# A planned kernel on one core: new load and crossbar times for the planner, a wider spacing of the attention, and batch 1's gates chunk by chunk

## The chip, the core and the metric

The kernel runs on one core of a Trainium2 chip. A core has several engines that work side by side: TensorE (PE in the profile) for matmuls, VectorE (DVE), ScalarE (ACT), GpSimd (POOL) and SyncE (SP), and 16 DMA engines that move data. The metric is the time of one execution on the device, in microseconds (us). The span of the profile is some 1.8 us shorter than that time.

The kernel before takes 193.66 us (median of four runs, 193.41 to 194.00).

## The reference

Four batches, eight heads, 768 steps, head size 48. A gated linear attention feeds an MLP-mixer:

```python
f = 1.0 / (1.0 + np.exp(-f_logit))
for t in range(S):                                     # S = 768
    state = f[:, :, t, :, None] * state + np.einsum('bhd,bhe->bhde', k[:, :, t], v[:, :, t])
    y[:, :, t] = np.einsum('bhd,bhde->bhe', q[:, :, t], state)
x = y, heads side by side                              # (4, 768, 384), shortened here
h = np.maximum(x.transpose(0, 2, 1) @ w_tok1, 0.0) @ w_tok2     # token mixing, 768 -> 256 -> 768
u = x + h.transpose(0, 2, 1)
out = u + np.maximum(u @ w_ch1, 0.0) @ w_ch2                    # channel mixing, 384 -> 1536 -> 384
```

Batch after batch, the kernel does the attention in six chunks of 128 steps and then the mixing. The channel mixing holds most of the matmul time. The attention of batch b + 1 is woven into the mixing of batch b.

## The kernel before

The order of the kernel's operations is not written down by hand. Each operation is handed to a `Plan` with the engine (or the engines) that can do it, the time that it is believed to take, what it waits for, and a priority, `key`. `order()` then plays the whole kernel through with these believed times and yields one list, and the operations are emitted in this order. On the chip each engine's queue works through its own part of the list from front to back. So a believed time changes no arithmetic and no duration. It changes which operation stands before which, on every engine, and which of two possible engines gets an operation.

```python
class Plan:
    # time between the end of an operation and its result being seen elsewhere
    LATE = {"PE": 0.32, "ACT": 0.24, "DVE": 0.24, "POOL": 0.3, "SP": 0.1, "Q": 2.0}
    ...
    def order(self):
        queues = {e: sorted((o for o in self.ops if e in o["eng"]), key=lambda o: o["key"])
                  for e in ("PE", "ACT", "DVE", "POOL", "SP", "Q")}
        ...
        while len(out) < len(self.ops):
            # of each engine: the operation that can start first, among those within
            # 0.02 us of it the one of the smallest key; of all engines, the earliest of these
            ...
            ends[n] = t + o["eng"][e]
            visible[n] = ends[n] + self.LATE[e]
```

"Q" stands for the DMA engines together: one channel on which transfers follow each other. A load by GpSimd is two operations, the issue on GpSimd's queue and the transfer on Q. A crossbar transpose (the DMA engines turn a tile; used in place of a matmul against the identity for q and k from batch 2's fifth chunk on, and for the mixing of batches 2 and 3) is an issue on SyncE and, before the change, 0.7 us on Q too.

```python
def load_f(b, key, at=0.0):           # the gate's input of a whole batch, batches 1 to 3
    m = swdge(lambda e: nc.gpsimd.dma_start(out=f_sb[i], in_=src), key, 2.28, 5.9, 0.3, ...)
def load_qkv(b, c, key, at=0.0):      # q, k, v of one chunk: three loads
    made[name, b, c] = swdge(lambda e, ...: nc.gpsimd.dma_start(...), key, 0.89, 0.71, 1.0, ...)
def crossbar(dst, src, key, deps):
    n = add({"SP": 1.2}, lambda e: nc.sync.dma_start_transpose(out=dst, in_=src), key, deps)
    return add({"Q": 0.7}, None, key, [n])

def gates(b, c0, c1, key):            # of n chunks at once
    cost = 0.08 + 0.33 * n
    a = add({"ACT": cost}, ... Exp ...)                         # profile: L255
    h = add({"ACT": cost}, ... Lhi = Ln, bf16 ...)              # L257
    g = add({"ACT": cost}, ... Ln, fp32 ...)                    # L259
    o = add({"POOL": 0.85 * n, "DVE": 0.4 * n + 0.08},          # Llo, L261: GpSimd or VectorE,
            lambda e: on(e).tensor_tensor(lo, fb, hi, ALU.subtract), key, [g, h])   # as the plan picks

LEAD = (-0.05, 0.11)                  # where attention stands among the mixing's keys
PACE = (33.0, 4.5)                    # attention of chunk m not before 33.0 + 4.5 m us
for b in range(B):
    # loads of batch b + 1 (from b = 1 on)
    ...
    n = 2
    for c in range(0, NCH, n):
        gates(b + 1, c, c + n, b + 0.85 + LEAD[0] + LEAD[1] * c)
        for a in range(c, c + n):
            attention(b + 1, a, b + 1.0 + LEAD[0] + LEAD[1] * a, PACE[0] + PACE[1] * (NCH * b + a))
    mixing(b, b + 1.0, 1.0)
order = plan.order()
```

Lines that the profile names below: L237 a load of q, k or v; L246 the crossbar; L331 the scores (q times k), which need both turned tiles; L371 and L376 the readout; L407 and L426 token mixing; L461 and L480 channel mixing; L188 and L190 copies on ScalarE and VectorE. The tiles: f_sb is the gate, Lhi its negative logarithm in bf16 and Llo the rest that bf16 left out; kh and qh are the scaled k and q, kT and qT the same turned; x_bf is the attention's result, which token mixing reads; u_bf and its turned uT feed the channel mixing, zT is its hidden layer; pA, py, pm and others that begin with p are results of matmuls.

Of the kernel before, what the change touches and what calls it, by code (L numbers as in the profile page):

```python
# [14 lines left out]
class Plan:  # L15



    LATE = {"PE": 0.32, "ACT": 0.24, "DVE": 0.24, "POOL": 0.3, "SP": 0.1, "Q": 2.0}
    BANKS = {"att": 5, "mix": 3}  # L20
    WINDOW = 150

# [3 lines left out]
    def add(self, engines, fn, key, deps=(), bank=None, frees=None, at=0.0, banks=1):  # L26
        n = len(self.ops)
        self.ops.append(dict(n=n, eng=engines, fn=fn, key=(key, n), deps=[d for d in deps if d is not None],
                             bank=bank, banks=banks, readers=[], at=at))
        if frees is not None:  # L30
            self.ops[frees]["readers"].append(n)
            self.ops[n]["deps"].append(frees)
        return n

    def order(self):
        queues = {e: sorted((o for o in self.ops if e in o["eng"]), key=lambda o: o["key"])
                  for e in ("PE", "ACT", "DVE", "POOL", "SP", "Q")}
        free = dict.fromkeys(queues, 0.0)
        ends, visible, on = {}, {}, {}
        taken = {b: [] for b in self.BANKS}  # L40
        out = []

        def earliest(o, e):
            t = max(free[e], o["at"])
            for d in o["deps"]:
                if d not in ends:
                    return None
                t = max(t, ends[d] + 0.05 if on[d] == e and e != "Q" else visible[d])
            if o["bank"]:
                t_ = taken[o["bank"]]  # L50
                k = len(t_) - self.BANKS[o["bank"]]
                for k_ in range(max(k, 0), k + o["banks"]):
                    for r in self.ops[t_[k_]]["readers"]:
                        if r not in ends:
                            return None
                        t = max(t, visible[r])
            return t

        while len(out) < len(self.ops):
            best = None  # L60
            for e, q in queues.items():
                while q and q[0]["n"] in ends:
                    q.pop(0)
                found, seen = [], 0
                for o in q:
                    if o["n"] in ends:
                        continue
                    seen += 1
                    if seen > self.WINDOW:
                        break  # L70
                    t = earliest(o, e)
                    if t is not None:
                        found.append((t, o))
                if not found:
                    continue
                t0 = min(t for t, _ in found)
                t, o = min(((t, o) for t, o in found if t <= t0 + 0.02), key=lambda f: f[1]["key"])
                if best is None or t < best[0]:
                    best = (t, o, e)
            t, o, e = best  # L80
            n = o["n"]
            ends[n] = t + o["eng"][e]
            visible[n] = ends[n] + self.LATE[e]
            on[n] = e
            free[e] = ends[n]
            if o["bank"]:
                taken[o["bank"]] += [n] * o["banks"]
            out.append((t, e, o))
        return out
# [3 lines left out]
def kernel(  # L93
# [12 lines left out]
    nc = tc.nc  # L106
# [30 lines left out]
    w_tok1 = st([128, NCH, DT], BF16, "w_tok1")  # L137
# [7 lines left out]
    f_sb = two([128, H, NCH, D], FP32, "f_sb")  # L145
# [34 lines left out]
    add = plan.add  # L180
    made = {}
# [21 lines left out]
    def swdge(fn, key, cost, us, units, deps, at=0.0):  # L203

        room, ring = 6.5 - units, []
        for m, u in reversed(issued):
            room -= u
            if room < 0:
                ring = [m]
                break  # L210
        n = add({"POOL": cost}, fn, key, list(deps) + ring, at=at)
        m = add({"Q": us}, None, key, [n])
        issued.append((m, units))
        return m

    def load_f(b, key, at=0.0):
        i = b % 2
        src = f_logit[b].rearrange("h (c t) d -> t h c d", t=C)
        if b == 0:
            for c in range(NCH):  # L220

                held = [] if c < 3 else [add({"DVE": 0.07}, lambda e, c=c: nc.vector.memset(
                    f_sb[i][0:1, 0, c, 0:1], 0.0), key + 0.06 * c, [], at=1.9 * c - 0.2)]
                n = add({"SP": 0.05}, lambda e, c=c: nc.sync.dma_start(out=f_sb[i][:, :, c, :], in_=src[:, :, c, :]),
                        key + 0.06 * c, held)
                made["f", b, c] = add({"Q": 1.1}, None, key + 0.06 * c, [n])
        else:
            m = swdge(lambda e: nc.gpsimd.dma_start(out=f_sb[i], in_=src), key, 2.28, 5.9, 0.3,
                      [made.get(("lo", b - 2, c)) for c in range(NCH)], at)
            for c in range(NCH):  # L230
                made["f", b, c] = m

    def load_qkv(b, c, key, at=0.0):
        i = b % 2
        for name, dst, src, users in (("q", q_sb, q, ("qh",)), ("k", k_sb, k, ("kh",)), ("v", v_sb, v, ("y", "d"))):
            made[name, b, c] = swdge(
                lambda e, dst=dst, src=src: nc.gpsimd.dma_start(out=dst[i][:, c], in_=chunk_of(src, b, c)),  # L237
                key, 0.89, 0.71, 1.0, [made.get((u, b - 2, c)) for u in users], at)

    def load_w(name, dst, src, key, us, units):  # L240
        made[name] = swdge(
            lambda e: nc.gpsimd.dma_start(out=dst, in_=src.rearrange("(kt p) n -> p kt n", p=128)),
            key, 0.85, us, units, [])

    def crossbar(dst, src, key, deps):
        n = add({"SP": 1.2}, lambda e: nc.sync.dma_start_transpose(out=dst, in_=src), key, deps)  # L246
        return add({"Q": 0.7}, None, key, [n])

    def gates(b, c0, c1, key):
        i, n = b % 2, c1 - c0  # L250
# [136 lines left out]
    def mixing(b, key0, span):  # L387
        i = b % 2
# [80 lines left out]
        for tt in range(NCH):  # L469
            t = {}  # L470
            kk = key(2.0)
            if b + 1 < B and tt >= NCH - 2:
                kk = key0 + span + 0.12
            half = None
            for k0 in (0, NCC // 2):
                def ch2(e, tt=tt, k0=k0, t=t):
                    if k0 == 0:
                        t["p"] = bank("mix", "pm")
                    for kt in range(k0, k0 + NCC // 2):
                        nc.tensor.matmul(t["p"][:, 0:DM], lhsT=zT[:, kt, tt * 128:(tt + 1) * 128],  # L480
                                         rhs=w_ch2[:, kt, :], start=(kt == 0), stop=(kt == NCC - 1))
                n = add({"PE": 0.99}, ch2, kk,
                        [half, made["w_ch2"]] + [made["z", b, tt // 3, kt] for kt in range(NCC)],
                        bank="mix" if k0 == 0 else None)
                first = n if k0 == 0 else first
                half = n
            made["c2", b, tt] = half
            o = out_sb[tt]
            n = made["o", b, tt] = add({"DVE": 0.47}, lambda e, tt=tt, t=t, o=o: nc.vector.tensor_tensor(  # L489
                o, u_nat[i][:, tt, :], t["p"][:, 0:DM], ALU.add),  # L490
                kk, [half, made.get(("out", tt))], frees=first)
            s = add({"SP": 0.1}, lambda e, tt=tt, o=o: nc.sync.dma_start(out=out_b[tt], in_=o), kk, [n])
            made["out", tt] = add({"Q": 0.7}, None, kk, [s])

    W2 = 5
    FIRST = 0.3
    XBAR_QK = 16
    XBAR_U = 2
    LEAD = (-0.05, 0.11)
    PACE = (33.0, 4.5)  # L500

    load_f(0, 0.0)
    load_qkv(0, 0, 0.0)
# [4 lines left out]
    made["masks"] = add({"POOL": 1.4}, masks, 0.0)  # L508
    for c in range(1, NCH):
        load_qkv(0, c, 0.1 * c)  # L510
    load_w("w_tok1", w_tok1, moe_w_tok1, 0.60, 3.0, 0.75)
    load_w("w_tok2", w_tok2, moe_w_tok2, 0.61, 2.2, 0.25)
    load_f(1, 0.615)
    load_w("w_ch1", w_ch1, moe_w_ch1, 0.62, 6.0, 0.4)
# [7 lines left out]
    for b in range(B):  # L522
        if b + 1 < B:
            for c in range(NCH):
                if b >= 1:
                    if c == 0:
                        load_f(b + 1, b + 0.05)
                    load_qkv(b + 1, c, b + 0.05 + 0.1 * c)
            n = 2
            for c in range(0, NCH, n):  # L530
                gates(b + 1, c, c + n, b + 0.85 + LEAD[0] + LEAD[1] * c)
                for a in range(c, c + n):
                    attention(b + 1, a, b + 1.0 + LEAD[0] + LEAD[1] * a, PACE[0] + PACE[1] * (NCH * b + a))
        mixing(b, b + 1.0, 1.0)
# [43 lines left out]
```

## Time and profile before

| | before |
|---|---|
| time, median of 4 runs | 193.66 us |
| span | 192.0 us |
| PE busy | 170.5 us (89%) |
| first channel-mixing matmul | 42.60 us |
| PE idle, 48 to 162 us | 3.4 us |

The page's first two parts, for the kernel before. Each digit is the busy share, or the granted TensorE clock, in tenths in one of 40 slices of 4.8 us:

```profile
PE 170.5 (89%) x1668; PEld 105.4 (55%) x1668; DVE 129.5 (67%) x286; ACT 129.4 (67%) x292; POOL 81.0 (42%) x92
PE   0787896679999999999999899999998999999992
PEclk9999999957999999999999999999999999999999
```

PE is the bound from the tenth slice on. What it loses lies in the first nine: the attention of batch 0, fed by loads, and then batch 0's token mixing, where the clock falls too. One caution belongs to the clock row: its first record falls where the matmuls become fast, and before it the row shows full clock although the matmuls run at half rate. In this trace the first record is at 24.8 us. The two 128x384 matmuls of a chunk's cumulative sum start 0.27 to 0.30 us apart in batch 0's later chunks, up to 24.1 us, and 0.17 us apart from 48.5 us on.

The stretches by engine, kernel before. The columns are the stretch, its length, the busy time and number of instructions of PE, PEld, DVE, ACT and POOL, the mean granted clock, the mean busy share of the DMA engines (3.15 means 3.15 of 16) and GB/s:

```profile
36.00:42.00 6.00, 3.44 (x28) 1.91 (x27) 5.51 (x10) 5.32 (x9) 4.11 (x3) 0.70 2.04 144
42.00:48.00 6.00, 6.00 (x65) 3.85 (x63) 4.94 (x11) 4.89 (x14) 6.00 (x8) 0.73 1.76 93
...
96.00:102.00 6.00, 6.00 (x77) 3.77 (x76) 5.91 (x14) 5.89 (x14) 5.26 (x7) 1.00 3.15 130
102.00:108.00 6.00, 4.99 (x41) 2.69 (x40) 5.09 (x13) 5.81 (x14) 0.16 (x1) 1.00 2.04 93
108.00:114.00 6.00, 6.00 (x61) 3.70 (x59) 4.47 (x10) 4.62 (x10) 1.48 (x1) 1.00 0.37 74
114.00:120.00 6.00, 6.00 (x48) 3.80 (x47) 3.03 (x6) 1.46 (x3) 0.00 (x0) 1.00 0.42 112
```

Between 36 and 42 us PE works 3.44 of 6 us, at a clock of 0.70. That is the hole which the change is aimed at.

Two pieces of the chain of waits, kernel before (start, duration, what):

```profile
101.08 6.33 DMA kT_92<-kh_88
107.85 1.57 PE pm L461 x9
```

And PE's wait for that transpose in the view of waits (total us, times, longest):

```profile
PE pA_1824 L331 <- DMA kT_92<-kh_88: 0.7, 1, 0.7
```

The transpose took 6.33 us from issue to landing (the median of the kernel's 28 is 2.42).

### The profile page before, as it was taken

The numbers are of one execution on the slowest core, as the hardware profiler recorded it, in microseconds if no ns is written. First come the engines' busy times: TensorE is split into PE (matmuls) and PEld (weight loads), VectorE is DVE, ScalarE is ACT, GpSimd is POOL, SyncE is SP. The second block draws the span as 40 slices with busy tenths as digits, with TensorE's granted clock in tenths as the row PEclk, the third lists the DMA queues.
The fourth block names the chain that finished last, engine by engine and source line by source line (L and its number), as shares of the span: only waits on it lengthen the run. The fifth ranks groups of instructions, "written<-read, shape, count | busy, mean of one in ns | idle before, by whom it ended". The sixth has DMA issues, their size and how long they took to land.

```text
span 192.0 us, 4351 instructions
## 1 busy us (share of the span) xinstructions
PE 170.5 (89%) x1668; PEld 105.4 (55%) x1668; DVE 129.5 (67%) x286; ACT 129.4 (67%) x292; POOL 81.0 (42%) x92
## 2 busy tenths in 40 slices
PE   0787896679999999999999899999998999999992
PEld 0455553346666666656555566565665654656560
DVE  4578888988899757988998973898673637200222
ACT  4999793987989959774899953257996122598000
POOL 7999992199992449993990300000000000000000
PEclk9999999957999999999999999999999999999999
DMA  8999999999999999999999343344532124310222
GB/s 105 162 149 143 141 216 194 196 101 107 112 192 195 167 122 171 180 199 155 180 144 115 58 82 113 103 85 130 84 64 48 41 85 100 78 70 2 81 86 82
DMA packets 102213, 23.23 MB, mean 121 GB/s; under 512 B 95312, under 2 KB 100992, under 8 KB 102192
## 3 DMA queue, kind: packets, MB, share of 16 engines
q0 software_dynamic: 78800, 13.77, 99.6%
q1 hardware_dynamic: 23392, 9.18, 21.1%
q8 instruction: 13, 0.21, 0.5%
q14 instruction: 8, 0.07, 0.1%
HBM read 25.17 MB, written 4.72 MB: 156 GB/s over the span
## 4 chain that ended last, share of the span: by engine, by line
PE 53%; DVE 18%; ACT 15%; DMA 6%; issue 4%; POOL 2%; DVEq 0%; POOLq 0%; ACTq 0%
PE pm L480 24%; PE pm L461 14%; DMA kT_92<-kh_88 3%; PE pm L407 3%; DMA k_sb_72<-in_k_dram 3%; PE pm L426 2%; ACT zT L194 2%; DVE u_bf L190 2%; PE py L371 1%; ACT state_bd_103 L188 1%; DVE Am_96 L337 1%; DVE Am_95 L337 1%; DVE u_nat_109 L430 1%; ACT u_bf L188 1%; ACT state_bd_102 L188 1%
## 5 line engine op out<-in xcount | busy, mean ns | idle before, releaser
L461 PE MATMUL pm<-uT,w_ch_68 128*128 128x384 bf16 x288 | 54.5, 330 | 1.1 <-ACT zT L194 0.8
L480 PE MATMUL pm<-w_ch_69,zT 128*128 128x384 bf16 x288 | 50.5, 326 | 0.0
L194 ACT ACTIVATE zT<-pm 128x384 bf16<-128x384 f32 x73 | 34.7, 500 | 6.2 <-PE pm L461 5.8
L480 PEld LDWEIGHTS <-zT 128*128 128x128 bf16 x288 | 27.3, 98 | 17.7 <-issue 0.4
L461 PEld LDWEIGHTS <-w_ch_68 128*128 128x128 bf16 x288 | 26.3, 98 | 17.2 <-issue 2.6
L237 POOL DMA_DIRECT2D k_sb_72<-in_k_dram x12 | 11.0, 920 | 4.9 <-DMA f_sb_76<-in_f_logit_dram 4.9
L237 POOL DMA_DIRECT2D q_sb_70<-in_q_dram x12 | 11.2, 932 | 4.4 <-DMA w_ch_69<-in_moe_w_ch_dram 3.6
L196 DVE TENSOR_SCALAR zT<-pm 128x384 bf16<-128x384 f32 x23 | 12.2, 551 | 1.2 <-PE pm L461 1.2
L237 POOL DMA_DIRECT2D k_sb_73<-in_k_dram x12 | 11.2, 932 | 3.7 <-DVE zT L196 3.7
L426 PE MATMUL pm<-h1T,w_tok_67 128*128 128x384 bf16 x48 | 10.9, 332 | 0.8 <-ACT h1T L194 0.4
L237 POOL DMA_DIRECT2D v_sb_75<-in_v_dram x12 | 11.3, 941 | 0.0
L237 POOL DMA_DIRECT2D v_sb_74<-in_v_dram x12 | 11.1, 926 | 0.4 <-issue 0.4
L237 POOL DMA_DIRECT2D q_sb_71<-in_q_dram x12 | 11.2, 936 | 0.0
L261 POOL TENSOR_TENSOR Llo_81<-f_sb_77,Lhi_79 128x768 bf16<-128x768 f32 x3 | 5.0, 1669 | 14.7 <-ACT f_sb_77 L259 14.7
L489 DVE TENSOR_TENSOR out_sb_114<-u_nat_110,pm 128x384 f32<-128x384 f32 x2 | 1.1, 550 | 14.1 <-PE pm L480 14.1
L274 PE MATMUL pS<-Lhi_78,tri_bf 128*128 128x384 bf16 x12 | 4.9, 409 | 4.8 <-POOL ident masks.py:197 4.8
L188 ACT CAST x_bf_106<-py 128x384 bf16<-128x384 f32 x10 | 4.8, 482 | 6.4 <-PE py L376 6.4
L190 DVE COPY x_nat_105<-py 128x384 f32<-128x384 f32 x8 | 4.5, 558 | 6.5 <-ACT x_bf_107 L188 6.4
L188 ACT CAST x_bf_107<-py 128x384 bf16<-128x384 f32 x8 | 3.9, 488 | 7.3 <-PE py L376 7.2
L190 DVE COPY x_nat_104<-py 128x384 f32<-128x384 f32 x9 | 5.0, 558 | 5.4 <-ACT x_bf_106 L188 5.4
L287 ACT ACTIVATE G_82<-pS 128x384 bf16<-128x384 f32 x12 | 5.9, 488 | 4.2 <-PE pS L281 4.1
L430 DVE TENSOR_TENSOR u_nat_109<-x_nat_104,pm 128x384 f32<-128x384 f32 x12 | 6.2, 550 | 3.6 <-PE pm L426 3.5
(237 smaller groups left out, 394.8 us busy)
## 6 DMA issues: line engine op xcount, KB each, us to landing
f_sb_77<-in_f_logit_dram POOLq DMA_DIRECT2D x2, 1152.0 KB, 12.1
f_sb_76<-in_f_logit_dram SPq DMA_DIRECT2D x6, 192.0 KB, 4.5
q_sb_70<-in_q_dram POOLq DMA_DIRECT2D x12, 96.0 KB, 5.7
k_sb_72<-in_k_dram POOLq DMA_DIRECT2D x12, 96.0 KB, 5.2
v_sb_74<-in_v_dram POOLq DMA_DIRECT2D x12, 96.0 KB, 5.2
w_ch_68<-in_moe_w_ch_dram POOLq DMA_DIRECT2D x1, 1152.0 KB, 15.5
q_sb_71<-in_q_dram POOLq DMA_DIRECT2D x12, 96.0 KB, 7.9
k_sb_73<-in_k_dram POOLq DMA_DIRECT2D x12, 96.0 KB, 6.1
```

What stands on the lines that cost most here:

```text
L188: nc.scalar.copy(dst, src)
L190: on(e).tensor_copy(dst, src)
L194: nc.scalar.activation(dst, src, AF.Relu, bias=0.0, scale=1.0)
L196: nc.vector.tensor_scalar(dst, src, 0.0, None, ALU.max)
L237: lambda e, dst=dst, src=src: nc.gpsimd.dma_start(out=dst[i][:, c], in_=chunk_of(src, b, c)),
L261: lambda e: on(e).tensor_tensor(lo, fb, hi, ALU.subtract), key, [g, h])
L287: return lambda e: nc.scalar.activation(dst.rearrange("t h d -> t (h d)"), t["pS"][:, 0:DM], AF.Exp, bias=0.0, scale=scale)
L407: nc.tensor.matmul(t["p"][:, 0:DM], lhsT=w_tok1[:, kt, rt * 128:(rt + 1) * 128], rhs=x_bf[i][:, kt, :], start=(kt == 0), stop=(kt == NCH - 1))
L426: nc.tensor.matmul(t["p"][:, 0:DM], lhsT=w_tok2[:, kt, tt * 128:(tt + 1) * 128], rhs=h1T[:, kt, :], start=(kt == 0), stop=(kt == 1))
L430: u = made["u", b, tt] = add({"DVE": 0.47}, lambda e, tt=tt, t=t: nc.vector.tensor_tensor(u_nat[i][:, tt, :], x_nat[i][:, tt, :], t["p"][: ...
L461: nc.tensor.matmul(t["p"][:, 0:384], lhsT=w_ch1[:, kt, cc * 128:(cc + 1) * 128], rhs=uT[:, kt, th * 384:(th + 1) * 384], start=(kt == 0), ...
L480: nc.tensor.matmul(t["p"][:, 0:DM], lhsT=zT[:, kt, tt * 128:(tt + 1) * 128], rhs=w_ch2[:, kt, :], start=(kt == 0), stop=(kt == NCC - 1))
```

## The change

Its intent is to let the planner believe what the profile measured (loads and crossbar), and to close the hole in batch 0's token mixing: batch 1's gates, which were done two chunks at a time in the middle of it, go chunk by chunk and later.

```diff
-    LATE = {"PE": 0.32, "ACT": 0.24, "DVE": 0.24, "POOL": 0.3, "SP": 0.1, "Q": 2.0}
+    LATE = {"PE": 0.32, "ACT": 0.24, "DVE": 0.24, "POOL": 0.3, "SP": 0.1, "Q": 2.0, "X": 1.3}
-                  for e in ("PE", "ACT", "DVE", "POOL", "SP", "Q")}
+                  for e in ("PE", "ACT", "DVE", "POOL", "SP", "Q", "X")}
     # load_f
-            m = swdge(..., key, 2.28, 5.9, 0.3,
+            m = swdge(..., key, 2.28, 6.3, 0.3,
     # load_qkv
-                key, 0.89, 0.71, 1.0, ...
+                key, 0.89, 0.78, 1.0, ...
     # crossbar
-        return add({"Q": 0.7}, None, key, [n])
+        return add({"X": 0.1}, None, key, [n])
     # store of the output
-            s = add({"SP": 0.1}, ...
+            s = add({"SP": 0.45}, ...
-    LEAD = (-0.05, 0.11)
-    PACE = (33.0, 4.5)
+    LEAD = (-0.05, 0.13)
+    PACE = (34.0, 5.6)
-    load_w("w_tok1", w_tok1, moe_w_tok1, 0.60, 3.0, 0.75)
+    load_w("w_tok1", w_tok1, moe_w_tok1, 0.60, 3.3, 0.75)
-            n = 2
+            n = 2 if b else 1
-                gates(b + 1, c, c + n, b + 0.85 + LEAD[0] + LEAD[1] * c)
+                gates(b + 1, c, c + n, b + (0.85 if b else 0.95) + LEAD[0] + LEAD[1] * c)
```

Below, its four parts have letters: **D**, the load times (f, q/k/v, w_tok1); **X**, the crossbar on a channel of its own, with its latency and the store's cost; **P**, LEAD and PACE; **G**, the gates of batch 1.

More of the change, by code (lines that the diff above doesn't have):

```diff
@@ L227, in load_f @@
         else:
-            m = swdge(lambda e: nc.gpsimd.dma_start(out=f_sb[i], in_=src), key, 2.28, 5.9, 0.3,
+            m = swdge(lambda e: nc.gpsimd.dma_start(out=f_sb[i], in_=src), key, 2.28, 6.3, 0.3,
                       [made.get(("lo", b - 2, c)) for c in range(NCH)], at)
@@ L237, in load_qkv @@
                 lambda e, dst=dst, src=src: nc.gpsimd.dma_start(out=dst[i][:, c], in_=chunk_of(src, b, c)),
-                key, 0.89, 0.71, 1.0, [made.get((u, b - 2, c)) for u in users], at)
+                key, 0.89, 0.78, 1.0, [made.get((u, b - 2, c)) for u in users], at)
     def load_w(name, dst, src, key, us, units):
@@ L491, in mixing @@
                 kk, [half, made.get(("out", tt))], frees=first)
-            s = add({"SP": 0.1}, lambda e, tt=tt, o=o: nc.sync.dma_start(out=out_b[tt], in_=o), kk, [n])
+            s = add({"SP": 0.45}, lambda e, tt=tt, o=o: nc.sync.dma_start(out=out_b[tt], in_=o), kk, [n])
             made["out", tt] = add({"Q": 0.7}, None, kk, [s])
```

## The prediction

> **What bounds it now.** TensorE: the page gives PE 170.5 us busy of 192.0 (89%), VectorE and ScalarE 67% each; the chain of waits is 53% PE. In stretches of 6 us PE is full from 48 us on: 3.4 us idle until 162 us, nothing until 188, then a tail of 3.7 us. What is lost lies before: 0 to 32 us (batch 0's attention, fed by loads; nearly unchanged) and 32 to 46 us, batch 0's token mixing. There, by stretches of 1 us, PE idles 3.7 us (32 to 42), and the granted clock is 0.72, 0.50 for six microseconds, then 0.86: 3.4 us of clock lost. The Trainium skill ("TensorE: Matmul & The Clock Gate", Part 1) says that the clock halves after an idle window of about 3.4 us; the trace agrees: the drop follows 35 to 38 us with PE 0.48, 0.54, 0.33 busy.
>
> **Why that hole.** Batch 1's gates come in blocks of two chunks, 0.83 us an instruction on ScalarE. The timeline shows nine of them from 34.0 to 42.4 us, 7.3 us of work, before or between the copies that token mixing needs. f for batch 1 landed at 34.0 us, and ScalarE stood 0.9 us waiting for it: the planner had believed it earlier. VectorE carries the mixing almost alone (u_nat, u_bf, uT; one u_bf took 1.74 us while GpSimd ran Llo). The first channel-mixing matmul starts at 42.6 us, though token mixing's second product began at 33.2.
>
> **What changes.** No arithmetic goes. (a) Loads are believed 10% slower and f 0.4 us slower, so batch 1's f is planned about 2 us later: copies come first. (b) Batch 1's gates go in single chunks (0.52 us alone, about 0.43 in a row) with later keys; they cost ScalarE some 0.5 us more in all, but block no copy for 0.8 us. (c) The crossbar gets its own channel: in the trace 1.2 us of SyncE each and 2.4 us to landing, 6 us where it met loads at 101 us; it was planned near 4. (d) Attention is paced 5.6 us a chunk in place of 4.5, away from 42 to 66 us (ScalarE and VectorE 80 to 98% busy) towards emptier stretches (114 to 126 us: ScalarE 1.5 to 2.4 of 6).
>
> **What it is worth.** Token mixing's own work is about 4 us on each of two engines plus 2 us of latency, so the first channel matmul should start near 38.5 to 39.5 us: 3 to 4 us gained (estimate from the durations above). If PE stays warm, 1.5 us more. Later stages hold at most 3.4 us; I expect between +0.5 and -1 us there, as the postponed gates load a nearly full ScalarE, and a crossbar planned too early makes PE wait. Sum: -4.7 us.
>
> **Prediction:** 189.2 us, 8 in 10 between 186.5 and 192.2. Faster by over 2% (below 190.0) 0.57, within 2% 0.40, slower 0.03.
>
> **What would show it.** First channel-mixing matmul at or before 39.5 us; mean granted clock between 36 and 48 us above 0.85 (now 0.72); ScalarE's gates between 34 and 40 us halved; PE busy down 2 to 4 us, since cold matmuls go; first crossbar transpose later than 97.6 us; batch 3's last readout (148 us) not earlier; idle PE between 48 and 162 us unchanged within 1.5 us.
>
> **What would make it wrong.** The clock drops all the same, as token mixing alone keeps PE half busy. The hole moves: batch 1's attention starts late and ScalarE, with the gates, bounds 44 to 66 us. Late pacing leaves too little work to cover batch 3's token mixing near 150 to 160 us. Or a reordered head loses what the mixing wins.

## More of the kernel before

GpSimd's timeline near 100 us, kernel before (start, duration, engine, line, operation; in brackets the idle time before it and what ended it):

```profile
99.43 0.96 POOL L237 DMA_DIRECT2D k_sb_73<-in_k_dram  x1
100.30 0.97 POOL L237 DMA_DIRECT2D v_sb_75<-in_v_dram  x1
107.84 1.64 POOL L261 TENSOR_TENSOR Llo_81<-f_sb_77,Lhi_79 128x768 bf16<-128x768 f32 x1 [6.58 <-ACT f_sb_77 L259]
```

The last loads of batch 3's q, k and v are issued by 101.3 us. GpSimd then waits 6.58 us for ScalarE before its next Llo (of batch 3's chunks 2 and 3; the one of chunks 0 and 1 ran on VectorE, at 101.54 us), and nothing stands behind it. A wait like this costs nothing.

## The result and the profile after

| | before | after |
|---|---|---|
| time, median of 4 runs | 193.66 us | 203.20 us |
| range | 193.41 to 194.00 | 202.74 to 203.27 |
| span | 192.0 us | 201.0 us |
| first channel-mixing matmul (L461) | 42.60 us | 44.42 us |
| mean clock, 36 to 48 us | 0.72 | 0.86 |
| PE idle, 102 to 120 us | 1.0 us | 5.4 us |
| last readout with the state (L376) | 151.9 us | 161.8 us |

The ratio is 1.049 (95% interval 1.046 to 1.051): the change is slower by 4.9%. Here and below, a ratio is the mean time of one kernel's fast runs over that of the other's fast runs in the same rounds, so it is not quite the ratio of the medians.

The first parts of the page, kernel after (slices of 5.0 us):

```profile
PE 174.6 (87%) x1668; PEld 106.8 (53%) x1668; DVE 132.8 (66%) x295; ACT 127.3 (63%) x295; POOL 80.3 (40%) x92
PE   0687797879999999989977499999899999999992
PEclk9999999699999999999999579999999999999999
```

The dip of the clock in the mixing is smaller (one slice at 6 in place of 5 and 7), and a new hole stands in slices 21 to 23, with the clock low behind it. The same stretches as above, kernel after:

```profile
36.00:42.00 6.00, 5.17 (x33) 2.74 (x33) 5.12 (x12) 4.46 (x12) 0.91 (x1) 0.72 1.92 169
42.00:48.00 6.00, 4.95 (x59) 3.28 (x56) 5.81 (x14) 6.00 (x18) 5.46 (x7) 1.00 1.35 73
...
96.00:102.00 6.00, 6.00 (x77) 3.81 (x76) 5.24 (x11) 5.28 (x11) 0.91 (x1) 1.00 0.43 20
102.00:108.00 6.00, 4.55 (x43) 2.60 (x41) 5.89 (x13) 4.77 (x12) 6.00 (x8) 1.00 1.63 68
108.00:114.00 6.00, 2.07 (x24) 1.14 (x22) 2.18 (x7) 2.98 (x7) 4.25 (x4) 0.79 2.21 117
114.00:120.00 6.00, 6.00 (x35) 3.18 (x34) 3.84 (x8) 2.89 (x6) 0.00 (x0) 0.64 0.52 52
```

Between 102 and 120 us PE idles 1.45 + 3.93 = 5.38 us, and the clock takes 2.07 x 0.21 + 6.00 x 0.36 = 2.59 us more: 7.97 us, against 1.01 us before. So 7.0 of the 9.0 us of span are lost in these 18 us.

To place the rest, I added up the matmul work issued by a given time, each matmul counted with its full-clock stream time (0.163 us for 384 columns, 0.056 for 128, 0.043 for 96, 0.025 for 48 and less). The kernel after is behind by 2.1 us at 36 us, by 0.1 at 48, by 0.7 at 102, by 7.7 at 120 and by 8.8 at 180. In words: the head lost 2.1 us, the token mixing won 2.0 us, the hole took 7.0 us, and 1.7 us went elsewhere.

**The head.** The attention of batch 0 was no aim of the change, but it got later. The last copy of batch 0's attention on ScalarE, kernel before and kernel after, in the timeline:

```profile
31.79 0.48 ACT L188 CAST x_bf_106<-py 128x384 bf16<-128x384 f32 x1 [0.72 <-PE py L376]
```

```profile
35.52 0.48 ACT L188 CAST x_bf_106<-py 128x384 bf16<-128x384 f32 x1 [3.08 <-PE py L376]
```

The token-mixing matmuls around it show that TensorE had become fast by 28 us before (4 matmuls in 0.82 us) and not after (5 in 1.81 us). First the kernel before, then the kernel after:

```profile
28.09 0.82 PE L407 MATMUL pm<-x_bf_106,w_tok_66 128*128 128x384 bf16 x4
```

```profile
28.95 1.81 PE L407 MATMUL pm<-x_bf_106,w_tok_66 128*128 128x384 bf16 x5
```

**The hole.** GpSimd's timeline, kernel after:

```profile
93.63 0.89 POOL L237 DMA_DIRECT2D v_sb_75<-in_v_dram  x1
101.09 1.63 POOL L261 TENSOR_TENSOR Llo_81<-f_sb_77,Lhi_79 128x768 bf16<-128x768 f32 x1 [6.56 <-ACT f_sb_77 L259]
102.67 0.92 POOL L237 DMA_DIRECT2D q_sb_71<-in_q_dram  x1
...
109.64 0.96 POOL L237 DMA_DIRECT2D v_sb_75<-in_v_dram  x1
```

In the new plan the Llo of batch 3's first two chunks stands on GpSimd in front of nine loads of q, k and v. The planner believed that ScalarE's Ln for it would be done at 95.9 us; ScalarE, busy 5.28 of the 6 us from 96 to 102, started it at 100.14. So GpSimd stood 6.56 us, and the nine loads behind it stood too. The Trainium skill says in "TensorE: Matmul & The Clock Gate" (section "Architectural detail") that ScalarE and VectorE are strict first-in-first-out queues, and GpSimd one for each of its cores; this trace agrees: no load went past the waiting Llo. The DMA engines are nearly empty from 96 to 102 us (0.43 of 16, 20 GB/s; before 3.15 and 130 GB/s). The loads that should have run then are issued from 102.67 to 110.6 us and meet the crossbar transposes of batch 2's last chunks. From the chain of waits, kernel after:

```profile
106.45 0.31 DVE zT L196
106.76 6.47 DMA kT_92<-kh_88
...
113.89 0.43 PE pm L461
```

And the wait for it, kernel after:

```profile
PE pA_1836 L331 <- DMA kT_92<-kh_88: 3.9, 1, 3.9
```

A landing of 6.47 us is no news: before it was 6.33. New is that PE's queue now had the scores right behind the transposes, because the planner believed the turned tile to be there 2.7 us after the start of the issue (1.2 for the issue, 0.1 until it is seen, 0.1 on X, 1.3 until that is seen). Before, it was 4.0 us (1.2 + 0.1 + 0.7 + 2.0) plus whatever was queued on Q. PE ran out of work at 109.35 us and stood until 113.28:

```profile
108.70 0.65 PE L461 MATMUL pm<-uT,w_ch_68 128*128 128x384 bf16 x3
113.28 0.29 PE L331 MATMUL pA_1836<-qT_90,kT_92 48*128 48x128 bf16 x1 [3.93 <-DMA kT_92<-kh_88]
```

The clock then fell to half for 6.8 us, from 111.5 us on. The Trainium skill ("TensorE: Matmul & The Clock Gate", Part 1) gives an idle window of about 3.4 us, 3413 ns, as the cause of a fall. The length agrees: the low phases in the clock records of all traces last multiples of 3.41 us, but for the last of each trace, which the end cuts off. That the window must be idle does not agree: this fall came 2.1 us after PE ran out of work, and PE had been busy 38% of the 3.41 us before it. The fall at 38.45 us in the kernel before, of which the prediction speaks, followed 3.41 us with PE busy 44%.

The late Llo slowed VectorE too. The Trainium skill ("SBUF — State Buffer", section "Who interferes with whom") says that a VectorE instruction with two inputs in SBUF contends with a GpSimd instruction that reads SBUF, and this trace agrees: the state update (L358), normally 0.36 us, took 1.79 us at 101.14 us, while Llo ran 1.63 us from 101.09. 1.31 us of it stand on the chain of waits.

So far this is a reading of one trace. Two causes, the held loads and the early scores, are named in it, and experiments were made to tell them apart.

### The profile page after: what moved, and what is told of

Its sections match the earlier page's. It is cut to its first block, busy times and chain, and to the rows that moved or that the text cites. A ratio compares the mean times of both kernels' runs of the same rounds, so it can differ in the third digit from the quotient of the medians.

```text
span 201.0 us, 4327 instructions
## 1 busy us (share of the span) xinstructions
PE 174.6 (87%) x1668; PEld 106.8 (53%) x1668; DVE 132.8 (66%) x295; ACT 127.3 (63%) x295; POOL 80.3 (40%) x92
## 4 chain that ended last, share of the span: by engine, by line
PE 53%; DMA 15%; DVE 14%; ACT 10%; issue 3%; POOL 3%; DVEq 0%; POOLq 0%; ACTq 0%
PE pm L480 24%; PE pm L461 13%; DMA f_sb_77<-in_f_logit_dram 6%; PE pm L407 4%; DMA kT_92<-kh_88 3%; ACT zT L194 3%; DMA k_sb_72<-in_k_dram 2%; PE py L371 2%; DMA k_sb_73<-in_k_dram 2%; PE pm L426 2%; DMA kT_93<-kh_89 2%; DVE Am_97 L337 2%; PE py L376 2%; DVE u_nat_109 L430 1%; DVE Am_95 L337 1%
## 5 line engine op out<-in xcount | busy, mean ns | idle before, releaser
L461 PE MATMUL pm<-uT,w_ch_68 128*128 128x384 bf16 x288 | 54.3, 333 | 0.4 <-ACT zT L194 0.2
L480 PE MATMUL pm<-w_ch_69,zT 128*128 128x384 bf16 x288 | 51.7, 330 | 0.0
L194 ACT ACTIVATE zT<-pm 128x384 bf16<-128x384 f32 x68 | 32.4, 496 | 11.0 <-PE pm L461 10.7
L461 PEld LDWEIGHTS <-w_ch_68 128*128 128x128 bf16 x288 | 26.4, 99 | 17.1 <-issue 2.3
L196 DVE TENSOR_SCALAR zT<-pm 128x384 bf16<-128x384 f32 x28 | 14.9, 549 | 2.2 <-PE pm L461 2.2
L426 PE MATMUL pm<-h1T,w_tok_67 128*128 128x384 bf16 x48 | 11.6, 361 | 0.8 <-ACT h1T L194 0.4
L261 POOL TENSOR_TENSOR Llo_81<-f_sb_77,Lhi_79 128x384 bf16<-128x384 f32 (+1 forms) x4 | 5.2, 1293 | 17.7 <-ACT f_sb_77 L259 17.7
L489 DVE TENSOR_TENSOR out_sb_114<-u_nat_110,pm 128x384 f32<-128x384 f32 x2 | 1.1, 552 | 14.1 <-PE pm L480 14.1
L188 ACT CAST x_bf_106<-py 128x384 bf16<-128x384 f32 x8 | 3.8, 478 | 8.9 <-PE py L376 8.9
L261 DVE TENSOR_TENSOR Llo_80<-f_sb_76,Lhi_78 128x384 bf16<-128x384 f32 (+1 forms) x8 | 5.6, 706 | 5.3 <-ACT f_sb_76 L259 5.2
L430 DVE TENSOR_TENSOR u_nat_109<-x_nat_104,pm 128x384 f32<-128x384 f32 x12 | 6.3, 550 | 3.5 <-PE pm L426 3.3
L188 ACT CAST x_bf_107<-py 128x384 bf16<-128x384 f32 x9 | 4.3, 482 | 6.2 <-PE py L376 6.1
L430 DVE TENSOR_TENSOR u_nat_110<-x_nat_105,pm 128x384 f32<-128x384 f32 x12 | 6.1, 545 | 2.7 <-PE pm L426 2.7
## 6 DMA issues: line engine op xcount, KB each, us to landing
f_sb_76<-in_f_logit_dram SPq DMA_DIRECT2D x6, 192.0 KB, 4.5
```

Of the source, the lines that this page charges most:

```text
L188: nc.scalar.copy(dst, src)
L194: nc.scalar.activation(dst, src, AF.Relu, bias=0.0, scale=1.0)
L196: nc.vector.tensor_scalar(dst, src, 0.0, None, ALU.max)
L426: nc.tensor.matmul(t["p"][:, 0:DM], lhsT=w_tok2[:, kt, tt * 128:(tt + 1) * 128], rhs=h1T[:, kt, :], start=(kt == 0), stop=(kt == 1))
L430: u = made["u", b, tt] = add({"DVE": 0.47}, lambda e, tt=tt, t=t: nc.vector.tensor_tensor(u_nat[i][:, tt, :], x_nat[i][:, tt, :], t["p"][: ...
L461: nc.tensor.matmul(t["p"][:, 0:384], lhsT=w_ch1[:, kt, cc * 128:(cc + 1) * 128], rhs=uT[:, kt, th * 384:(th + 1) * 384], start=(kt == 0), ...
```

## The experiments

Twelve kernels were run, each beside the kernel before on the same chip. All gave the reference's result. Two of a1's four runs were over 1.5% above its fastest and count as slow; all other runs that are used here are fast. "Lead" is the matmul work issued by a given time less that of the kernel before, as above. In the traces of the experiments, the tile names have no number.

### a1: the loads back in front of Llo, nothing else

After the plan is made, the nine loads are moved ahead of the Llo in the list. Only GpSimd's queue changes its order.

```diff
     order = plan.order()
+    lo = made["lo", 3, 1]
+    at = next(i for i, (t, e, o) in enumerate(order) if o["n"] == lo)
+    loads = {made[x, 3, c] - 1 for c in range(NCH) for x in "qkv"}
+    rest = order[at:]
+    order = order[:at] + [f for f in rest if f[2]["n"] in loads] + [f for f in rest if f[2]["n"] not in loads]
```

> The changed kernel with one thing moved: on GpSimd the nine q/k/v loads of batch 3 (chunks 3 to 5) stand in front of the subtraction Llo of batch 3's first two chunks, not behind it; no other queue changes its order. Theory (the held-back loads collide with batch 2's crossbar transposes): the loads are issued near 94.5 to 102.5 us, the 3.9 us wait of TensorE for kT at 109 to 113 us falls under 1 us, the granted clock stays 1.0 between 108 and 120 us, and the time falls from 203.2 to about 195.5 us (194 to 197.5). Rival (the planner's new belief in a short crossbar, or the late pace, makes TensorE wait whatever GpSimd does): the wait stays above 3 us, the time stays within 1.5 us of 203.

Measured: 194.32 and 196.91 us in its two fast runs (median of all four 197.51), ratio 1.008 (0.997 to 1.018), against 1.049 of the whole change. The loads are issued from 94.33 to 102.2 us. Kernel a1, in the same stretch as above and in the view of waits:

```profile
108.00:114.00 6.00, 6.00 (x54) 3.64 (x53) 5.44 (x11) 2.99 (x6) 0.88 (x1) 1.00 0.44 87
```

```profile
PE pA L331 <- DMA kT<-kh: 2.0, 2, 1.0
```

The hole is gone and the clock stays at 1.00. Holding the loads is therefore a necessary part of it. The trace is of a1's fastest run; the four scatter over 4.8 us, but the slowest (199.13) is still 3.6 us under the change's fastest. A note on the scatter: up to 92 us a1 and the change have the same queues, yet token mixing's first ten second-product matmuls took 2.15 us in a1's trace and 3.16 us in the change's, where the clock was low. Such differences between runs of one order move these kernels by a microsecond or more.

### a4: the mirror, in the kernel before

The kernel before, with the same Llo moved to GpSimd and in front of the same nine loads.

```diff
     order = plan.order()
+    lo = made["lo", 3, 1]
+    at = next(i for i, (t, e, o) in enumerate(order) if o["n"] == lo)
+    order[at] = (order[at][0], "POOL", order[at][2])
+    loads = {made[x, 3, c] - 1 for c in range(3, NCH) for x in "qkv"}
+    ahead = order[:at]
+    order = ([f for f in ahead if f[2]["n"] not in loads] + [order[at]]
+             + [f for f in ahead if f[2]["n"] in loads] + order[at + 1:])
```

> The kernel before with the mirror of the first run: the Llo of batch 3's first two chunks goes from VectorE to GpSimd, and stands there in front of the nine loads of batch 3's chunks 3 to 5. Theory: GpSimd waits until about 101 us for ScalarE, the loads follow until 110 us and collide with the crossbar transposes issued from 101 to 112 us, which take over 5 us to land; TensorE waits over 3 us for them, time 197 to 202 us. Rival (the collision needs the changed beliefs and pace): under 195.5 us.

Measured: 194.58 us (194.48 to 195.75), ratio 1.004 (0.998 to 1.009). This is a miss, and a useful one. The loads were held until 103.90 us, even longer than in the change, and transposes took up to 6.1 us to land. Yet in the view of waits, kernel a4:

```profile
PE pA L331 <- DMA kT<-kh: 1.8, 1, 1.8
```

PE lost only 1.4 us between 102 and 120 us. In this kernel's order, planned with the longer belief about the crossbar, PE had other work before the scores. Held loads alone do not make the hole.

### b2: the change, with batch 2's last tiles turned by TensorE

The loads stay held, but nothing that PE waits for goes through the DMA engines in that stretch.

```diff
-    def crossbar(dst, src, key, deps):
+    def crossbar(dst, src, key, deps, name=None):
+        if name:            # batch 2, chunks 4 and 5: four matmuls against ident, and a copy
+            def turned(e):
+                p = bank("att", name)
+                for hp in range(HP):
+                    nc.tensor.matmul(p[:, hp * 128:(hp + 1) * 128], lhsT=src[:, hp * 128:(hp + 1) * 128],
+                                     rhs=ident, start=True, stop=True)
+                copy("ACT" if name == "pq" else "DVE", dst, p.rearrange("p (a t) -> p a t", a=4))
+            n = add({"SP": 1.2}, None, key, deps)
+            return add({"X": 0.1}, turned, key, [n])
```

> The changed kernel in its own order, the nine loads still held behind Llo, but the four crossbar transposes of batch 2 (chunks 4 and 5) done by TensorE (4 matmuls against the identity and one copy each, as for the earlier chunks). Theory (the hole is the crossbar transposes meeting the held-back loads): TensorE's wait near 109 us falls from 3.9 to under 1 us, clock 1.0 there, the held-back loads alone cost at most 2 us, time 195 to 198.5 us. Rival (it is the loads' own lateness that starves the attention of batch 3, the crossbar is only where it shows): a hole of 3 us or more stays between 108 and 120 us, time above 200 us.

Measured: 197.39 us (196.57 to 198.29), ratio 1.020 (1.013 to 1.027). GpSimd's timeline and the stretch, kernel b2:

```profile
101.57 1.64 POOL L270 TENSOR_TENSOR Llo<-f_sb,Lhi 128x768 bf16<-128x768 f32 x1 [6.61 <-ACT f_sb L268]
103.16 0.92 POOL L237 DMA_DIRECT2D q_sb<-in_q_dram  x1
```

```profile
108.00:114.00 6.00, 5.61 (x62) 3.45 (x60) 5.49 (x13) 4.90 (x11) 4.71 (x5) 1.00 1.89 97
```

L270 is L261 here, nine lines further down. GpSimd waits as in the kernel after (6.61 us), and PE works 5.61 of 6 us at full clock. The lead falls by 1.1 us between 102 and 120 us in place of 7.0. So the hole is PE waiting for the crossbar. It is not PE lacking q, k or v of batch 3.

### b1: the change without its crossbar part (D, P, G)

The crossbar is believed as before: on Q, 0.7 us and 2.0 until seen. The plan still puts Llo in front of the nine loads.

```diff
-        return add({"X": 0.1}, None, key, [n])
+        return add({"Q": 0.7}, None, key, [n])
```

(and the channel X and the store's 0.45 taken out)

> The change without its crossbar part (crossbar latency and store cost as before). This plan still has the Llo in front of the nine loads, but places the score matmuls later behind their transposes. Theory (both are needed: held loads and scores placed 2.6 us behind their transposes): transposes take up to 6 us to land as in the changed kernel, but TensorE waits under 2 us for them, time 196 to 200 us. Rival (held loads alone suffice): wait over 3.5 us, time 201 to 205 us.

Measured: 204.68 us (204.19 to 206.31), ratio 1.059 (1.051 to 1.068). At the place in question the theory held, and the test is cleaner there than it was planned to be. In the traces, the first 1013 matmuls of b1 and of the kernel after stand in the same order, up to these scores, and so do the instructions of the other engines up to that point. The loads are held (Llo waits 6.2 us), and the transpose takes 6.69 us to land. But 47 matmuls stand between its issue and the scores, in place of 20, and PE does not wait. Kernel b1, SyncE and PE:

```profile
105.45 1.21 SPq L246 DMA_TRANSPOSE kT<-kh  x1
110.13 3.08 PE L480 MATMUL pm<-w_ch,zT 128*128 128x384 bf16 x18
113.15 0.40 PE L331 MATMUL pA<-qT,kT 48*128 48x128 bf16 x8
```

In the stretch PE is busy at full clock:

```profile
108.00:114.00 6.00, 5.51 (x40) 2.99 (x38) 4.03 (x9) 4.46 (x10) 1.26 (x2) 1.00 2.04 135
```

But the total was missed by far, and lies in the rival's range: the kernel is even slower than the whole change. It has other holes, 3.5 us between 132 and 138 us (VectorE waits 6.0 us for a transposed qT from 135.4 us on) and 6.5 us between 168 and 180 us. The view of waits, kernel b1:

```profile
PE pm L461 <- DMA uT<-u_bf: 5.4, 2, 3.8
```

So the short belief makes this hole, and yet the new crossbar times cannot be called the culprit of the total: with the other parts in place, the order without them is worse. What a1, a4, b2 and b1 show together, for the stretch of 102 to 120 us:

| kernel | loads held | crossbar believed short | turned by the crossbar | lost there |
|---|---|---|---|---|
| after | yes | yes | yes | 7.0 us |
| a1 | no | yes | yes | 0.0 us |
| a4 | yes | no | yes | 1.4 us |
| b1 | yes | no | yes | 0.8 us |
| b2 | yes | yes | no | 1.1 us |

Among these five kernels, the large hole is there only where all three come together. a1 and b2 change one thing against the kernel after. b1 has its order up to the scores in question, so at this place it too changes one thing, where the scores stand. These three are the strong evidence. They leave no room for the slowed state update as the cause either: b1 and b2 have it (1.79 us at 99.82 and at 101.63) without the hole. a4 differs from the kernel after in its whole order, and only agrees.

### a2 and a3: the load times left out, and alone

> The change without its new load times (f 5.9, q/k/v 0.71, w_tok1 3.0 as before; crossbar, gates and pace as changed). The plan then leaves no Llo in front of those nine loads, and batch 0's attention is ordered as before. Theory: no hole near 108 us, batch 0's last x_bf near 32 us (35.5 in the changed kernel), time 188 to 192 us, so as fast as before or faster. Rival (crossbar belief or pace costs it): the hole stays, time above 198 us.

> The kernel before with only the new load times. Theory: the head gets the changed kernel's order, batch 0's last x_bf comes near 35.5 us in place of 31.8; no Llo stands in front of batch 3's loads, so no hole near 108 us; time 195 to 198 us (2 to 4 us slower than before). Rival (the load times are harmless, the other parts cost the time): 192.5 to 194.5 us.

a2 (X, P, G; the change less D): 193.19 us (192.42 to 193.75), ratio 0.996 (0.990 to 1.002). a3 (D alone): 196.01 us (195.76 to 197.37), ratio 1.011 (1.005 to 1.017).

a2's time misses the foretold 188 to 192 us; a3's lies in its range. a2 shows what the change was meant to do, and in batch 0's mixing it does it. The clock never drops in the mixing, and the first channel-mixing matmul comes at 39.84 us, kernel a2:

```profile
39.84 0.65 PE L461 MATMUL pm<-uT,w_ch 128*128 128x384 bf16 x3
```

At 48 us it leads by 3.0 us. Half of that is given back: between 48 and 60 us PE works 10.91 of 12 us, where VectorE and ScalarE are the bound (VectorE 18.4 of the 20 us from 46 to 66), and the lead is 1.4 us at 102. a3 has no hole near 110 us either, and a late head: its first channel-mixing matmul comes at 45.91 us. Thus no part alone is the cause of the hole; D only re-deals the queues.

### b3 and b4: the change without P, and without G

> The change without the new lead and pace. This plan has no Llo in front of the nine loads. Theory: no hole near 108 us, 194 to 198 us (the head keeps its loss of about 2 us). Rival (the crossbar belief alone makes the hole): wait for kT over 3 us, above 200 us.

> The change without the single-chunk gates of batch 1. No Llo in front of the nine loads either. Theory: no hole near 108 us; first channel-mixing matmul at 45 us or later, as in the run with the load times alone; 195 to 199 us. Rival (crossbar belief or late pace alone makes the hole): above 200 us.

b3 (D, X, G): 198.34 us (two runs, 198.28 and 198.40), ratio 1.025 (1.017 to 1.033). b4 (D, X, P): 198.72 us (198.49 and 198.95), ratio 1.027 (1.019 to 1.035). Neither has the large hole; b3 is 2.1 us behind the kernel before at 102 us and 4.4 at 180, b4 2.5 and 5.1 (lead; both are left out of the table below). b3's time lies 0.3 us above its foretold range, b4's in its range, with the first channel-mixing matmul at 46.43 us. So taking away any one of the four parts removes this hole; without X, other holes come in its place.

### c1, c2, c3: which load time matters

> The change with its new time for f (6.3) but with the old ones for q/k/v (0.71) and w_tok1 (3.0). The plan keeps the head of the kernel before and puts no Llo in front of the nine loads. Theory (of the load times only that of q/k/v does harm): 191 to 193.5 us, at or below the kernel before; no wait above 1.5 us for kT. Rival (any of the three load times does the harm): 195 us or more.

> The change with all its numbers, only the q/k/v time set back to 0.71. Theory (this one number reorders the head and, with gates and pace, puts the Llo in front of the nine loads): head as in the kernel before, no hole, 191.5 to 194.5 us against 203.2. Rival: above 196 us.

> Only the crossbar part and the gates, load times and pace as before. Theory: head as in the kernel before, token mixing with the gain of the single-chunk gates (first channel-mixing matmul near 40 us), no hole: 191 to 194 us. Rival (without the slower pace ScalarE and VectorE bound 44 to 66 us): 194.5 us or more.

```diff
  # c2: X, P, G, and of D only
-    ... key, 2.28, 5.9, 0.3,        # f
+    ... key, 2.28, 6.3, 0.3,
  # c3: the whole change, with q/k/v put back
-    ... key, 0.89, 0.78, 1.0,
+    ... key, 0.89, 0.71, 1.0,
  # c1: X and G only
```

c2: **192.01 us** (six runs, 190.77 to 192.45), ratio 0.989 (0.986 to 0.993). It has the lowest median, and its median and its waits for kT (1.0 us at most) are as foretold. By the ratio it is 1.1% under the kernel before, clear of the scatter. Its token mixing is as short as a2's, kernel c2:

```profile
40.14 0.65 PE L461 MATMUL pm<-uT,w_ch 128*128 128x384 bf16 x3
```

and between 102 and 120 us PE is busy all 18 us.

c3: 196.28 us (195.88 to 197.96), ratio 1.015 (1.010 to 1.019). With 0.71 in place of 0.78 for q/k/v the head is as before (lead -0.2 us at 36 us, not -2.1), the mixing gains 3.0 us by 48 us, and the hole is gone. So the head's loss is due to that one number. All the traces say so: the eight changed kernels with 0.78 are 1.8 to 2.5 us behind at 36 us, the five with 0.71 at most 1.0. The expected total was missed all the same, and lies where the rival put it: 2.2 us go between 84 and 90 us, about 1 between 120 and 126, and 2.4 between 162 and 168, where PE waits 1.8 us for a transposed uT.

c1: 194.77 us (193.89 to 196.17), ratio 1.006 (1.001 to 1.010). The time is that of the rival. The lead of 2.5 us at 48 us is down to 0.3 at 66. a2, which differs from c1 by P alone, still has 1.5 of its 3.0 us there, so the slower pace of the attention keeps part of the gain.

### d1: is it the place of the token-mixing matmuls that makes the head late?

In the change's order, ten cold matmuls of token mixing stand before the scores of batch 0's last chunk. d1 is a1 with these ten moved behind them.

```diff
+    early = [f for f in order if f[2]["fn"] is not None and f[2]["fn"].__name__ == "tok1"][:10]
+    order = [f for f in order if f not in early]
+    at = next(i for i, (t, e, o) in enumerate(order) if o["n"] == made["A", 0, 5])
+    order = order[:at + 1] + early + order[at + 1:]
```

> The first run of the study (loads in front of Llo) with a second move: on TensorE the ten early token-mixing matmuls of batch 0, which stand in two groups of five before the last scores of batch 0 (1.8 and 1.6 us at the low clock), go behind those scores. Theory (they hold up the last chunk of batch 0's attention): batch 0's last x_bf comes near 34 us in place of 35.5, and the time falls by about 1 us against the first run, to 193.5 to 197 us. Rival (the late gates of chunk 5 on ScalarE set the head, the matmuls only fill waiting time): x_bf stays within 0.5 us of 35.5 us, time as in the first run.

Measured: 197.85 us (196.71 to 198.89), ratio 1.019 (1.013 to 1.024). The theory fell, and the rival's time of x_bf was missed as well. Kernel d1, PE and ScalarE in the timeline:

```profile
32.92 3.38 PE L407 MATMUL pm<-x_bf,w_tok 128*128 128x384 bf16 x10
```

```profile
36.98 0.48 ACT L188 CAST x_bf<-py 128x384 bf16<-128x384 f32 x1 [4.65 <-PE py L376]
```

The last x_bf came even later (36.98 us), as the ten matmuls, still cold, now stood in front of the readout (in a1 it came at 34.82). So d1 only shifted their cost and does not clear them. That the q/k/v number makes the head late is shown (c3). By which of the re-dealt queues it does so stays open.

### The plan's own idea of the end

When it is built, the kernel computes when the planner believes it ends. This is not a measurement of anything; it is set beside the medians here:

```
kernel   plan believes   measured (us)
before       186.9           193.7
after        185.4           203.2
a2           185.0           193.2
a3           188.3           196.0
b1           192.1           204.7
b3           186.1           198.3
b4           190.0           198.7
c1           184.8           194.8
c2           184.8           192.0
c3           187.1           196.3
```

The change promised 1.5 us less and cost 9.5 us more. c1 and c2 promise the same and differ by 2.8 us.

And the lead in microseconds of matmul work, for the kernels that the argument uses (my own sum from the traces, as explained):

```
at us   after    a1    a2    a3    a4    b1    b2    c1    c2    c3    d1
   36    -2.1  -1.8  -0.5  -1.8  -0.3  -1.8  -2.1  -1.0  -0.8  -0.2  -2.5
   48    -0.1   1.0   3.0  -2.7  -0.6   1.0  -0.8   2.5   2.0   3.0  -1.3
  102    -0.7   0.8   1.4  -3.3  -0.6  -0.2  -1.3   0.0   1.1   0.9  -1.4
  120    -7.7   0.8   2.0  -2.6  -2.0  -1.0  -2.4   0.4   2.3   0.6  -3.0
  180    -8.8  -0.5   1.5  -2.1  -1.8 -10.9  -3.7  -0.7   1.6  -2.3  -4.6
```

## Why the prediction was wrong

The prediction said 189.2 us (186.5 to 192.2) and gave 0.03 to slower by over 2%. The kernel took 203.2 us.

**What was right.** The reading of the hole in batch 0's token mixing, and that this change can close it: a2, which has the gates and not the load times, starts the channel mixing at 39.84 us (foretold: 39.5 at the latest) with the clock up, and leads by 3.0 us at 48 us, as "3 to 4 us gained" said. Even in the kernel after the mean clock between 36 and 48 us rose from 0.72 to 0.86 (foretold: above 0.85), ScalarE's gates between 34 and 40 us fell from 5.63 to 1.91 us (foretold: halved; the late head has its part in it), and the first crossbar transpose came later, at 105.39 us in place of 97.60.

**The step that failed.** "Later stages hold at most 3.4 us; I expect between +0.5 and -1 us there." The 3.4 us were the idle time that the *old* order leaves after 48 us. It bounds what can still be won there. It does not bound what can be lost, because the diff makes a new order for every queue to the end of the kernel. The runs show 7.0 us lost between 102 and 120 us, in a place that no line of the diff names. The mechanism itself was half named ("a crossbar planned too early makes PE wait") and priced at under 1 us, from the old order, in which a transpose of 6.33 us cost PE 0.7. In the new order it cost 3.93 us at once, and the fall of the clock came on top; with the scores placed later behind the same slow transpose (b1) it cost nothing. The other half, a waiting Llo in front of nine loads on GpSimd, is not in the prediction: the trace before showed GpSimd waiting 6.58 us for ScalarE near that place, harmless there, with nothing queued behind it.

**The second error.** "0 to 32 us [...] nearly unchanged." The head lost 2.1 us by 36 us, which is why the first channel-mixing matmul was not at 39.5 us but at 44.42. c3 shows that the q/k/v time of 0.78 does it. The prediction listed it only as the last of its risks ("a reordered head loses what the mixing wins").

**The third.** Of the 3.0 us won in the mixing, a2 keeps 1.4 us at 102 us. The prediction named this too ("the hole moves [...] and ScalarE, with the gates, bounds 44 to 66 us") and did not take it off the sum. With the head unchanged and no hole, the sum would have been close to c2's and a2's 192 to 193 us: still a miss by three, for this term.

**The foretold signs.** PE busy was to fall by 2 to 4 us and rose by 4.1 (more matmuls ran cold). Idle PE was to stay within 1.5 us between 48 and 162 us; between 102 and 120 us alone it rose by 4.4. "Batch 3's last readout (148 us)" was misread: 148 us belongs to the other of the two alternating tiles, the last is at 151.9 us, and after the change at 161.8.

**What stays open.** Which queue in the head carries the q/k/v time's effect (d1 did not settle it), and why c3 and b1 lose where they do beyond the waits that were named.

## What to carry to other kernels

In a kernel whose order comes from a planner, a single believed time that is set closer to the profile need not make a better order: it re-deals every in-order queue, and the idle time of the old order is no bound for what the new one can lose. Before trusting such a change, list what stands behind each operation that waits, above all loads behind a computing operation on the queue that issues them, and what stands right behind each transfer's believed landing. Then take the parts one by one: here the change less two of its load times (q/k/v and w_tok1) is 1.1% faster than before, and the whole is 4.9% slower.

## What the Trainium skill lacked or had wrong

- "DMA: Bandwidth & Descriptors" (section "Rules for kernel authors") says that "A transpose next to ordinary DMAs needs nothing". As to correctness that holds: all runs were correct. As to time, a transpose of 128x512 bf16 landed 6.47 us after its issue beside nine loads, and 2.4 us at most other times; the page's transpose sections give no latency beside other traffic.
- "TensorE: Matmul & The Clock Gate" (Part 1) gives about 3.4 us of sustained work for the clock to rise, and an idle window of about that length for it to fall. It does not say how busy a window may or must be. For the rise: with PE busy 60 to 90% of most slices of the head, the first clock record came at 24.8 us (before), 33.0 us (after) and 38.0 us (d1). For the fall: the clock fell 14 times inside the spans of the 14 traces, each time after 3.41 us in which PE was 33 to 51% busy, with no idle stretch over 2.2 us in them.
